# A new spread of the work over the sections of a seven-product attention and mixture kernel, with independent last writes and a root for the first 1/rms

## The chip, the cores and the metric

The kernel runs on one core of a Trainium2 chip. The metric is the device time of one execution in microseconds (us). Three executions of the kernel before gave 538.40, 540.46 and 545.57 us; the time before is their median, 540.46 us.

## What is computed

The reference is an attention block with normed queries and keys, followed by a mixture-of-depths block over the concatenated heads (8 batches, 12 heads, 448 tokens, 64 channels each):

```
q_n, k_n = x / sqrt(mean(x*x) + 1e-6) * g          # for q and for k, per token and head
attn = softmax(q_n @ k_n.T / 8)                    # 448 x 448, for each of 96 heads
x[b, s, :] = concat over heads of attn @ v         # 448 x 768 per batch
scores = x[b] @ w_gate                             # one number per token
top = the 128 tokens with the highest scores       # per batch
out[b] = x[b]
out[b, top] += sigmoid(scores[top]) * (relu(x[b, top] @ w1) @ w2)    # 768 -> 1024 -> 768
```

All data are float32.

## The kernel before

**Attention.** The heads are worked in 24 groups of four heads, three groups to a batch (`n`, `q` in the code; counted from 0). A group has seven units, one for each 64 keys. A unit is `scores` (K times Q into two PSUM banks of the ring `ps_sc`, four banks in all), two `Exp` on ScalarE that write a tile `p`, and `values` (`p` times V, added up over the group in `ps_av`). The 1/rms of the keys is the scale operand of the `Exp`; that of the queries is multiplied into the transposed queries `qT` ahead of the group's first `scores`. For this, `squares` (ScalarE) and `sum_squares` (a sum on VectorE, a power of -0.5 on GpSimd, L263) give `rinv`, `rows_out` writes it to DRAM, `rows_in` reads it back spread over the partitions (`bc`), and `scale_q` (VectorE, L294) multiplies. `scores` of group n cannot start before `scale_q(n)`. Groups 0 and 1 use `scale_q_early`, which spreads `rinv` by small matmuls (L305).

**Denominators.** `add_probs` adds the `p` tiles of a group on VectorE (L375). `by_array(n)` says how many of the last tiles of a group are left to TensorE instead: `sum_keys` multiplies the sum and each of those tiles by `pick_pair` (L402). Then `invert_sums` transposes, takes reciprocals (`rden`, L418), and `to_tokens` turns the group's output to token order in two halves (transposes L433, multiplication by `rden` L435). The second half shares the one bank `ps_aux` with the denominators, so its transposes wait for `rden`.

**Gate and ranks.** `gate` (VectorE, L463, four products for each of two column ranges), `spread`, `score_rows`, `count` (L504) and `annotate` give each token its rank; `select` writes the 128 chosen rows to DRAM (GpSimd's queue, L531), and `load_selected` fetches them.

**Mixture.** Two batches are worked together with a seven-product (Strassen-like) form of both layers. `mixture(g)` is cut in 15 pieces: the transposes of the selected rows (L617), seven products of layer 1 (L649) and seven of layer 2 (L719). Sums of weight blocks are made once (`mix`, L242), stored to DRAM and fetched through a ring of three buffers. Results go out by indirect writes in GpSimd's queue (L574); the last pair of batches has four of them, and each waits for the one before.

**Order of work.** Each engine and each DMA queue takes its instructions in the order in which the program issues them; there is no scheduler. The loop over groups issues `scores` and `values`. Other work is put in a table by `at(slot, ...)` and issued by `run(upto)`; a slot is a unit's number. Groups 0 to 7 have two places for it, after units 3 and 6; from group 8 on, places lie after the group's units, with up to three mixture pieces between them. `urgent` holds `scale_q`, issued in the second half of the group before. After group 23, the rest of the pieces follow, `ranks_of(7)` among them.

## Time and profile before

| of the profiled execution | |
|---|---|
| its own time | 540.99 us |
| span, first to last instruction | 539.3 us |
| TensorE matmul busy | 490.4 us (91%) |
| VectorE busy | 361.3 us (67%) |
| ScalarE busy | 284.2 us (53%) |
| GpSimd busy | 188.1 us (35%) |
| mean granted TensorE clock | 0.972 |

The busy time of TensorE counts modelled ends of overlapping matmuls, so it says little on its own; a pause shows as idle time before a matmul, given in square brackets in the timeline together with what ended it. A wait put down to "issue" ended by nothing that the profile names. The granted clock is the share of the full TensorE clock in a stretch. A matmul of float32 leaves two records in the trace.

### The profile page before, as it was taken

Reading aid. Unit: us, or ns where it says so; the run is one execution under the profiler, and the core shown is the slowest. Engines: PE = TensorE matmul, PEld = TensorE weight load, DVE = VectorE, ACT = ScalarE, POOL = GpSimd, SP = SyncE. Lnnn points to the kernel's source line nnn. Section 1 sums busy time; section 2 is a strip of 40 time slices with the busy share of each in tenths; the row PEclk is TensorE's granted clock in tenths of the full one; section 3 lists DMA queues with packets and bytes.
Section 4 is the critical chain, followed back from the end, with each engine's and each line's share of the span. In section 5 each row is a group of like instructions: output and inputs, shape, how many; then the busy total and the mean of one; then the engine's idle time right before and its main releaser. Section 6 shows DMA issues by size and latency. Waiting matters only on the chain. (4 is left out here: it accounts for less than half of the span.)

```text
span 539.3 us, 12042 instructions
## 1 busy us (share of the span) xinstructions
PE 490.4 (91%) x4861; PEld 294.5 (55%) x4861; DVE 361.3 (67%) x638; ACT 284.2 (53%) x519; POOL 188.1 (35%) x105
## 2 busy tenths in 40 slices
...
GB/s 312 270 287 219 264 211 270 247 300 291 285 237 103 289 281 165 266 143 306 250 298 192 143 349 260 251 143 318 224 248 141 116 124 112 223 260 87 179 89 33
...
## 3 DMA queue, kind: packets, MB, share of 16 engines
...
## 5 line engine op out<-in xcount | busy, mean ns | idle before, releaser
L344 ACT ACTIVATE p<-sc,rinv 128x448 f32<-128x448 f32 x336 | 187.9, 640 | 108.6 <-PE sc L335 94.2
L263 POOL TENSOR_TENSOR rinv<-ss,neg_half 128x14 f32<-128x14 f32 (+1 forms) x49 | 134.0, 2737 | 216.5 <-DVE ss L262 147.7
L335 PE MATMUL sc<-qT,kT 64*64 64x448 f32 x1344 | 163.4, 552 | 15.7 <-issue 11.1
L359 PE MATMUL av<-p,v 64*64 64x448 f32 x1344 | 155.7, 542 | 0.0
L375 DVE TENSOR_TENSOR sum<-sum,p 128x896 f32<-128x896 f32 x91 | 99.2, 1090 | 17.5 <-ACT p L344 13.5
L335 PEld LDWEIGHTS sc<-qT,kT 64*64 64x64 f32 x1344 | 57.7, 134 | 84.4 <-issue 55.4
L359 PEld LDWEIGHTS av<-p,v 64*64 64x64 f32 x1344 | 62.7, 134 | 66.9 <-issue 60.4
L531 POOL DMA_INDIRECT selected<-x,rank x32 | 36.8, 1151 | 62.6 <-DVE x L523 54.8
L435 DVE TENSOR_TENSOR x<-x_ps,rden 112x512 f32<-112x512 f32 x48 | 32.8, 689 | 32.5 <-PE x_ps L433 30.5
L262 DVE TENSOR_REDUCE ss<-sq 128x14 f32<-128x910 f32 (+1 forms) x49 | 52.4, 1075 | 0.9 <-ACT sq L253 0.9
L253 ACT ACTIVATE sq<-tok 128x896 f32<-128x896 f32 (+1 forms) x49 | 45.1, 937 | 6.2 <-DMA tok<-in_tok_dram 5.1
L463 DVE SCALAR_TENSOR_TENSOR prod<-x,wg 112x448 f32<-112x448 f32 (+1 forms) x64 | 35.7, 558 | 2.1
L433 PE MATMUL x_ps<-ident,xT 128*112 128x128 f32 x192 | 29.6, 279 | 6.5 <-DVE rden L418 6.5
L375 DVE TENSOR_TENSOR sum<-p 128x896 f32<-128x896 f32 x24 | 26.1, 1087 | 10.0 <-ACT p L344 10.0
L294 DVE SCALAR_TENSOR_TENSOR qT<-qT,gg,bc 128x896 f32<-128x896 f32 x22 | 25.2, 1145 | 6.0 <-DMA bc<-rows 4.7
L433 PEld LDWEIGHTS x_ps<-ident,xT 128*112 128x112 f32 x192 | 21.7, 135 | 12.3 <-DVE rden L418 9.1
L504 DVE SCALAR_TENSOR_TENSOR cmp<-score_rows,gate,earlier 112x448 f32<-112x448 f32 x32 | 21.9, 684 | 9.8 <-ACT score_rows L494 8.9
L382 ACT COPY xT<-av 128x448 f32<-128x448 f32 x48 | 23.3, 538 | 9.4 <-PE av L359 9.1
L574 POOL DMA_INDIRECT out_dram<-xe,row x7 | 7.7, 1105 | 50.1 <-DVE xe L583 35.9
L649 PE MATMUL moe_ps<-xeT,ring 128*128 128x128 f32 x192 | 23.1, 277 | 0.9 <-DVE hT L666 0.9
L583 DVE SCALAR_TENSOR_TENSOR xe<-moe_ps,xe 128x384 f32<-128x384 f32 x14 | 8.6, 614 | 22.2 <-PE moe_ps L719 22.2
L649 PE MATMUL side_ps<-xeT,w 128*128 128x128 f32 x192 | 23.1, 277 | 0.0
...
## 6 DMA issues: line engine op xcount, KB each, us to landing
...
```

The source lines that it names most:

```text
L253: nc.scalar.activation(out=sq[:, h, :, 0:D], in_=t[:, h], func=AF.Square, scale=scale)
L262: nc.vector.tensor_reduce(out=ss[:, h], in_=sq[:, h], axis=AX.X, op=OP.add)
L263: nc.gpsimd.tensor_tensor(out=rinv[:, h].rearrange(flat), in0=ss[:, h].rearrange(flat), in1=neg_half.to_broadcast([128, (h.stop - h.start) ...
L335: nc.tensor.matmul(out=scs[hh][D * c : D * (c + 1), 0:S], lhsT=get("kT", n)[r, c, D * i : D * (i + 1)], rhs=get("qT", n)[r, c, :], start=True,
L344: nc.scalar.activation(out=p[:, hh], in_=scs[hh][:, 0:S], func=AF.Exp, scale=rinvs[n, 1][:, hh, i : i + 1],)
L359: nc.tensor.matmul(out=avs[n][c][D * hh : D * (hh + 1), 0:S], lhsT=get("v", n)[r, hh, i, :], rhs=probs[u][r, hh], start=(i == 0), stop=(i ...
L375: nc.vector.tensor_tensor(out=sums[n], in0=probs.pop(u - 1) if begins else sums[n], in1=probs.pop(u), op=OP.add)
L433: nc.tensor.transpose(out=ps[:CP, j, :], in_=t[:, j, :], identity=ident)
L435: nc.vector.tensor_tensor(out=xs[b][:, :, col : col + 128].rearrange("p j (h d) -> p j h d", d=D), in0=ps[:CP].rearrange("p j (h d) -> p j ...
L463: nc.vector.scalar_tensor_tensor(out=prod[:, 0 : cols.stop - cols.start], in0=xs[b][:, j, cols], scalar=1.0, in1=wg[:, cols], op0=OP.mult, ...
L531: w = nc.gpsimd.indirect_dma_start(out=t[:, :], out_offset=bass.IndirectOffsetOnAxis(ap=rank[:, j : j + 1], axis=0), in_=x[:, j, :], in_of ...
L649: nc.tensor.matmul(out=ps[:, 128 * f : 128 * f + n], lhsT=w[:, d, 128 * f : 128 * (f + 1)], rhs=h[:, d, :n], start=first and f == d == 0, ...
```

## The change

The tables at the top of the file now set the order. A slot is a group's number plus a fraction (0.5 and 0.9 for the two places of groups 0 to 7; 0.4, 0.6, 0.75 and 0.9 for those of the later groups).

- `scale_q(n)` moves from the second place of group n-1 to its first. `rows_in` follows `rows_out` directly. Loads, squares and sums get new slots.
- `ARRAY` replaces `by_array`: 14 tiles in all go through TensorE instead of 29, and so VectorE makes 106 additions `sum<-sum,p` instead of 91.
- The gate of batch 1 is worked out by TensorE (`pick_gate`, 8 matmuls for each of its groups, then one small multiplication); the 8 products on VectorE for that batch go.
- The weight mixing is spread by `MIXED` from slot 8.9 to 14.6; gates and rankings are cut in halves with slots of their own.
- The mixture starts in group 9, not 8 (`SKIP`); 34 of its 60 pieces are issued by the end of group 23's loop, before 36. In four groups (`OTHER_BANK`) the second half of `to_tokens` takes a bank of `ps_sc` instead of `ps_aux`.
- In layer 1 the result of product 5 is added from its copy in `hT`. In layer 2 of the first two pairs, product 3 comes ahead of 7.
- Of the last pair's writes, the third and fourth are declared independent of the others, and their row numbers are worked out on GpSimd just ahead of each.
- At the start, 1/rms of group 0 is a `Sqrt` on ScalarE, a reciprocal and one correcting step on VectorE, and no power on GpSimd; the first tokens are loaded by two queues, 12 matmuls of zeros run ahead of the branch and 9 warming transposes instead of 13 behind it; `scale_q_early(1)` is issued at the end of group 0 instead of its middle.

```diff
+ARRAY = (0, 0, 1, 2, 2, 1, 2, 2, 1, 0, 0, 2, 1, 0, 0, 0, 0, 0, 0, 0, 0, 0, 0, 0)
+GATE_PE = {1}
+OTHER_BANK = (12, 14, 15, 21)
+SKIP = ((8, 0), (8, 1), (8, 2), (11, 2), (13, 2), (14, 1), (17, 2), (18, 2), (19, 0), (19, 2),
+ (21, 1), (22, 1), (23, 1), (23, 2))
+MIXED = ((1, 1, 0, 8.9), (1, 1, 1, 9.3), (1, 2, 0, 9.6), (1, 2, 1, 10.3), (1, 3, 0, 10.3),
+ (1, 3, 1, 10.3), (1, 0, 0, 10.9), (1, 0, 1, 11.4), (2, 1, 0, 11.9), (2, 1, 1, 11.9),
+ (2, 2, 0, 12.3), (2, 2, 1, 12.6), (2, 3, 0, 12.6), (2, 3, 1, 13.9), (2, 0, 0, 13.9),
+ (2, 0, 1, 14.6))
+PREPARED = {5: {'sq1': 3.5, 'sum0': 2.92},
+ 6: {'scale': 5.5},
+ 7: {'out': 5.5},
+ 8: {'sum1': 6.9},
+ 10: {'in': 8.92},
...
         self.gcol = pool.tile([128, 2], F32, name="gcol", bufs=1)
+        self.load("tok", 0, 0)
         nc.scalar.dma_start(out=self.gcol, in_=g2)
         neg_half = pool.tile([128, 1], F32, name="neg_half", bufs=1)
         nc.vector.memset(neg_half, -0.5)
...
-        warm = pool.tile([128, 1], F32, name="warm", bufs=1)
-        nc.scalar.activation(out=warm, in_=neg_half, func=AF.Exp)
-        self.neg_half = neg_half
-        self.load("tok", 0, 0)
+        warm = pool.tile([128, 2], F32, name="warm", bufs=1)
+        nc.vector.memset(warm, 1.0)
+        nc.scalar.activation(out=warm[:, 0:1], in_=warm[:, 1:2], func=AF.Sqrt)
+        self.neg_half, self.warm = neg_half, warm
...
+        if (name, n, i) == ("tok", 0, 0):
+            for h, queue in enumerate((self.nc.scalar, self.nc.sync)):
+                queue.dma_start(out=t[:, h], in_=src[:, h])
+        else:
+            self.nc.sync.dma_start(out=t, in_=src)
...
+        ss = sss[0, i]
+        for h in [slice(0, 1), slice(1, 2)] if i == 0 else [slice(0, 2)]:
+            nc.vector.tensor_reduce(out=ss[:, h], in_=sq[:, h], axis=AX.X, op=OP.add)
+
+    def root_first(i):
+        root = norm_pool.tile([128, 2, NI], F32, name="ss", bufs=4)
+        nc.scalar.activation(out=root, in_=sss[0, i], func=AF.Sqrt)
+        return root
...
+        nc.vector.reciprocal(out=root, in_=root)
+        nc.vector.scalar_tensor_tensor(
+            out=rinv, in0=root, scalar=-0.5, in1=ss, op0=OP.mult, op1=OP.mult
+        )
+        nc.vector.tensor_tensor(out=rinv, in0=rinv, in1=root, op=OP.mult)
+        nc.vector.scalar_tensor_tensor(
+            out=rinv, in0=rinv, scalar=1.5, in1=root, op0=OP.add, op1=OP.mult
+        )
+        rinvs[0, i] = rinv
...
     def by_array(n):
 
-        return 2 if n < 14 else 1 if n == n_groups - 1 else 0
+        return ARRAY[n]
...
+        for c in range(2 if n // NG in GATE_PE else 0):
+            for j in range(NJ):
+                nc.tensor.matmul(
+                    out=ps[32 * j : 32 * (j + 1), 0:CP],
+                    lhsT=pick_gate[:, n % NG * 2 + c],
+                    rhs=xTs[n, c][:, j, :],
+                    start=False,
+                    stop=(c == 1),
+                )
...
+        rows, written = [], []
+
+        def find_row(engine, i, k):
...
         def write(i, k):
             c0, c1 = parts_out[i][k]
-            nc.gpsimd.indirect_dma_start(
+            if k > 0:
+                find_row(nc.gpsimd, i, k)
+            w = nc.gpsimd.indirect_dma_start(
                 out=out.flatten_outer_dims().rearrange("r (k c) -> (r k) c", c=c1 - c0),
                 out_offset=bass.IndirectOffsetOnAxis(ap=rows[i][:n, k : k + 1], axis=0),
                 in_=xe[i][:n, c0:c1],
                 in_offset=None,
             )
+            for other in written if k > 0 else ():
+                tc.declare_no_dep(w.ins, other.ins, reason="other columns or other rows")
+            written.append(w)
...
-    slot = [0]
-
-    urgent = {}
+    slot = [0.0]
+    A, END = 0.5, 0.9
+    MID, P0, P1, P2 = 0.4, 0.6, 0.75, 0.9
...
-        s2, s1 = NI * (n - 2), NI * (n - 1)
-        late_rows, late_scale = n - 2 >= FIRST, n - 1 >= FIRST
-        times = [s2 - 2, s2, s2 + 2, s2 + 5] if n > 2 else [0, 0, 5, 7]
+        times = {
+            "sq0": n - 3 + (END if n - 3 < FIRST else P0),
+            "sum0": n - 3 + END + 0.03 if n - 3 < FIRST else n - 2 + MID,
+            "sq1": n - 2 + A if n - 2 < FIRST else n - 2 + P0 if n - 3 < FIRST else n - 3 + P1,
+            "sum1": n - 2 + END + 0.02 if n - 2 < FIRST else n - 2 + MID,
+            "out": n - 2 + (A if n - 2 < FIRST else P0),
+            "in": n - 2 + (A if n - 2 < FIRST else P2),
+            "scale": n - 1 + (A if n - 1 < FIRST else P0),
+        }
...
+        for k, t in PREPARED.get(n, {}).items():
+            times[k] = t
         for i in range(2):
-            at(times[2 * i], lambda i=i: sq.setdefault(i, squares(n, i)))
-            at(times[2 * i + 1], lambda i=i: sum_squares(n, i, sq.pop(i)))
-        at(3 if n == 2 else s2 + 3 if late_rows else s2 + 4, rows_out, n)
-        at(5 if n == 2 else s2 + 5 if late_rows else s1, rows_in, n)
-        urgent[s1 + (2 if late_scale else 4)] = n
+            at(times[f"sq{i}"], lambda i=i: sq.setdefault(i, squares(n, i)))
+            at(times[f"sum{i}"], lambda i=i: sum_squares(n, i, sq.pop(i)))
+        at(times["out"], rows_out, n)
+        at(times["in"], rows_in, n)
+        at(times["scale"], scale_q, n)
...
-            at(max(s0 - 26, 4 * (n - 3)), load, "tok", n, 0)
-            at(max(s0 - 26, 4 * (n - 3)), load, "tok", n, 1)
+            for i in range(2):
+                at(n - 5 + P2 if n > 5 else (n - 3) * 0.6, load, "tok", n, i)
         if n > 1:
-            at(max(s0 - 13, 2), load, "qT", n)
-            at(max(s0 - 11, 2), load, "kT", n)
-            at(max(s0 - 11, 2), load, "v", n)
+            at(max(n - 3 + 0.1, 0.3), load, "qT", n)
+            at(max(n - 2 + A, 0.3), load, "kT", n)
+            at(max(n - 2 + A, 0.3), load, "v", n)
...
-            at(16 + 3 * (2 * k + part), load_block, l, b, part)
-    for k, (i, part) in enumerate([(1, 0), (1, 1), (2, 0), (2, 1), (3, 0), (3, 1)]):
-        first = NI * FIRST + k + (3 if i == 3 else 0)
-        at(first, mix, 1, i, part)
-        at(first + 3, store_mixed, 1, i, part)
...
+            at(2.3 + 0.43 * (2 * k + part), load_block, l, b, part)
+    for l, i, part, t in MIXED:
+        at(t, mix, l, i, part)
+        at(t + 0.25, store_mixed, l, i, part)
...
-    for i in range(2):
-        sum_squares(0, i, squares(0, i))
-    later = [squares(1, i) for i in range(2)]
+    sum_first(0, squares(0, 0))
+    root = root_first(0)
+    keys = squares(0, 1)
...
+    invert_first(0, root)
+    sum_first(1, keys)
+    root = root_first(1)
+    nc.scalar.activation(out=loads.warm[:, 0:1], in_=loads.warm[:, 1:2], func=AF.Exp)
     scale_q_early(0)
-    for i in range(2):
-        sum_squares(1, i, later[i])
-
...
     for q in range(n_groups):
         u0 = NI * q
...
                     for u in (i, i + 1):
                         if u in us:
                             scores(u0 + u)
+                        if u0 + u in following:
+                            sum_squares(*following[u0 + u], squares(*following[u0 + u]))
                     run_values(u0 + i - 1 if i < NI - 1 else u0 + i - 2, hold=i == us[2])
-                scale_queries(u0 + us[-1])
-                slot[0] = u0 + us[0]
+                slot[0] = q + (END if place else A)
                 if place == 0:
-                    if q == 0:
-                        scale_q_early(1)
...
+                    if q > NG and g == 1 and b - 1 in GATE_PE:
+                        ranks_of(b - 1)
+                elif q == 0:
+                    scale_q_early(1)
...
                 add_late()
-                run(u0 + us[-1])
+                run(q + (1 - 1e-6 if place else A))
...
                 if u < NI:
                     scores(u0 + u)
             run_values(u0 + i - 1 if i < NI - 1 else u0 + i - 2)
-            if i == 2 and g == 1 and b % 2 == 0:
-                slot[0] = u0 - 2
-                ranks_of(b - 1)
-                run(u0)
-        slot[0] = u0
+            if i == 2:
+                slot[0] = q + MID
+                run(q + MID)
+        slot[0] = q + P0
...
-        next(moe)
-        slot[0] = u0 + 2
-        scale_queries(u0 + 3)
+        run(q + P0)
+        step(q, 0)
+        slot[0] = q + P1
         invert_sums(q - 1)
         to_tokens(q - 1, 0, ps_sc)
-        run(u0 + 3)
-        if q not in (21, 23):
-            next(moe)
-        slot[0] = u0 + 4
-        to_tokens(q - 1, 1, ps_aux)
-        run(u0 + 6)
-        if q not in (10, 11, 13, 15, 17, 19) and q < 20:
-            next(moe)
-        run(u0 + 6)
+        run(q + P1)
+        step(q, 1)
+        slot[0] = q + P2
+        to_tokens(q - 1, 1, ps_sc if q in OTHER_BANK else ps_aux)
+        if g == 0 and b - 1 in GATE_PE:
+            ranks_of(b - 1)
+        run(q + P2)
+        step(q, 2)
...
+            zeros = pool.tile([128, 128], F32, name="zeros")
+            nc.gpsimd.memset(zeros, 0.0)
+            ps = psum.tile([128, 128], F32, name="warm_ps")
+            for _ in range(12):
+                nc.tensor.matmul(out=ps, lhsT=zeros, rhs=zeros, start=True, stop=True)
```

**VectorE in group 4.** `sum<-p` is the first addition of a group, `prod` the gate, `qT<-qT,gg,bc` is `scale_q(5)`, `rden` the reciprocals of the denominators. Before:

```order
L375 TENSOR_TENSOR sum<-p 128x896
L262 TENSOR_REDUCE ss<-sq_122 128x14
L463 SCALAR_TENSOR_TENSOR prod,gate_parts<-x,wg 112x320 x4
L476 TENSOR_REDUCE gate<-gate_parts 112x4
L480 TENSOR_SCALAR parts<-gate 112x4
L481 TENSOR_SCALAR parts<-gate 112x4
L375 TENSOR_TENSOR sum<-sum,p 128x896 x2
L294 SCALAR_TENSOR_TENSOR qT<-qT,gg,bc 128x896
L418 RECIPROCAL rden<-den_ps 112x4x2x2
```

And now:

```order
L435 TENSOR_TENSOR sum<-p 128x896
L354 SCALAR_TENSOR_TENSOR qT<-qT,gg,bc 128x896
L545 SCALAR_TENSOR_TENSOR prod,gate_sums<-x,wg 112x320 x4
L558 TENSOR_REDUCE gate<-gate_sums 112x4
L567 TENSOR_SCALAR parts<-gate 112x4
L568 TENSOR_SCALAR parts<-gate 112x4
L435 TENSOR_TENSOR sum<-sum,p 128x896 x2
L487 RECIPROCAL rden<-den_ps 112x4x2x2
```

`scale_q` stands ahead of the gate and of the two additions, no longer behind them; a sum of squares has left this place.

**TensorE after the last group.** `row_ps` is the start of the ranking of batch 7; `xeT_ps<-ident,p` needs the rows selected by it; each `moe_ps` or `side_ps` row is one product. Before:

```order
L488 MATMUL row_ps<-ident,gate 112x112 x4
L719 MATMUL side_ps<-w_10_179,hT 128x384 x4
L719 MATMUL moe_ps<-ring,xeT 128x384 x4
L719 MATMUL side_ps<-ring,xeT 128x384 x4
L719 MATMUL moe_ps<-ring,xeT 128x384 x4
L719 MATMUL side_ps<-w_11_180,hT 128x384 x4
L719 MATMUL moe_ps<-ring,hT 128x384 x4
L617 MATMUL xeT_ps<-ident,xe 128x128 x6
L617 MATMUL xeT_ps<-ident,p 128x128 x6
```

And now:

```order
L575 MATMUL row_ps<-ident,gate 112x112 x4
L744 MATMUL moe_ps<-xeT,ring 128x128 x12
L814 MATMUL moe_ps<-w_00_191,hT 128x384 x4
L814 MATMUL side_ps<-w_10_192,hT 128x384 x4
L814 MATMUL moe_ps<-ring,xeT 128x384 x4
L814 MATMUL side_ps<-ring,xeT 128x384 x4
L814 MATMUL moe_ps<-ring,xeT 128x384 x4
L814 MATMUL side_ps<-w_11_193,hT 128x384 x4
L814 MATMUL moe_ps<-ring,hT 128x384 x4
L720 MATMUL xeT_ps<-ident,xe 128x128 x6
L720 MATMUL xeT_ps<-ident,p 128x128 x6
```

Eight products stand between the two, before it were six.

**GpSimd's queue at the end,** with the semaphores that each row waits for. Before:

```order
L574 DMA out_dram<-xe,row_5322 3584x768 [waits DMASW7_49,DMASW6_49,DVE_49]
L574 DMA out_dram<-p,row_5334 7168x384 [waits DMASW7_49,DMASW4_49,DMASW0_49]
L574 DMA out_dram<-p,row_5334 10752x256 [waits DMASW1_49,DMASW0_49,DVE_49]
L574 DMA out_dram<-p,row_5334 21504x128 [waits DMASW2_49,DMASW1_49,DVE_49]
```

And now:

```order
L674 DMA out_dram<-xe,row_5261 3584x768 [waits DMASW7_49,DMAHW5_49,DMASW6_49,DVE_49]
L674 DMA out_dram<-p,row_5273 7168x384 [waits DMASW7_49,DMASW4_49,DMASW0_49]
L661 TENSOR_SCALAR row_5273<-p 128x1
L674 DMA out_dram<-p,row_5273 10752x256 [waits DMASW1_49,DVE_49,Pool_49]
L661 TENSOR_SCALAR row_5273<-p 128x1
L674 DMA out_dram<-p,row_5273 21504x128 [waits DMASW2_49,DVE_49,Pool_49]
```

The last two writes no longer wait for the semaphore of the write ahead of them; the second one still does, and a small instruction precedes each of the last two.

## Rows read from the trace of the kernel before

**Rows 1.** Busy time by stretch of the span: start:end, length, then for each engine the busy us and the number of records, the granted clock, the DMA engines' busy share and GB/s. The first four stretches are groups 0 to 7, 9 to 14, 15 to 22, and group 23 with what follows up to the last matmul.

```profile
core 0: us, PE busy (x) PEld busy (x) DVE busy (x) ACT busy (x) POOL busy (x), PEclk, DMA share, GB/s
11.00:134.30 123.30, 110.65 (x1340) 54.88 (x1340) 83.92 (x141) 86.45 (x155) 61.27 (x31) 0.99 0.81 264
155.00:285.20 130.20, 124.17 (x1261) 73.96 (x1259) 95.23 (x166) 70.61 (x129) 44.60 (x22) 0.97 0.71 238
285.20:433.70 148.50, 145.67 (x1396) 84.65 (x1395) 121.77 (x211) 90.78 (x168) 51.86 (x25) 1.00 0.65 213
433.70:525.10 91.40, 84.52 (x571) 62.32 (x570) 40.55 (x86) 19.16 (x37) 11.59 (x12) 0.96 0.46 153
...
304.00:325.20 21.20, 21.20 (x215) 14.59 (x214) 19.91 (x42) 13.70 (x25) 6.80 (x4) 1.00 0.95 331
68.60:87.00 18.40, 15.56 (x174) 7.76 (x174) 11.04 (x22) 11.34 (x21) 5.34 (x2) 0.91 0.73 223
484.40:490.00 5.60, 5.54 (x32) 5.54 (x33) 1.86 (x6) 0.96 (x2) 0.96 (x1) 0.61 0.19 75
```

**Rows 2.** Timeline of TensorE in group 3: start us, duration us, engine, line, operation, names, shapes, count of records.

```profile
53.38 1.71 PE L359 MATMUL av<-p,v 64*64 64x448 f32 x16
54.89 1.71 PE L335 MATMUL sc<-qT,kT 64*64 64x448 f32 x16
...
58.03 0.59 PE L402 MATMUL den_ps<-sum,pick_pair 128*32 128x112 f32 x16
58.44 0.95 PE L402 MATMUL den_ps<-p,pick_pair 128*32 128x112 f32 x32
```

**Rows 3.** Timeline of the first `scores` of groups 4, 5, 7 and 8 (the idle time before them in brackets), with the work on VectorE ahead of that of group 4.

```profile
65.17 2.28 DVE L375 TENSOR_TENSOR sum<-sum,p 128x896 f32<-128x896 f32 x2
67.37 1.15 DVE L294 SCALAR_TENSOR_TENSOR qT<-qT,gg,bc 128x896 f32<-128x896 f32 x1
68.62 1.58 PE L335 MATMUL sc<-qT,kT 64*64 64x448 f32 x8 [3.29 <-issue]
...
87.00 0.98 PE L335 MATMUL sc<-qT,kT 64*64 64x448 f32 x8 [2.82 <-issue]
...
117.96 1.31 PE L335 MATMUL sc<-qT,kT 64*64 64x448 f32 x9 [2.85 <-issue]
...
134.29 1.74 PE L335 MATMUL sc<-qT,kT 64*64 64x448 f32 x16 [2.16 <-issue]
```

**Rows 4.** Timeline: transposes of `to_tokens` that waited for the reciprocals, in groups 11 and 21.

```profile
222.68 1.10 PE L433 MATMUL x_ps<-ident,xT 128*112 128x128 f32 x4 [2.48 <-DVE rden L418]
...
415.02 0.65 PE L433 MATMUL x_ps<-ident,xT 128*112 128x128 f32 x4 [1.93 <-DVE rden L418]
```

**Rows 5.** Timeline after the last group: the ranking of batch 7, two products of layer 2 that follow each other, the last of the four writes of the selected rows, the matmuls that need them, and two products of layer 1.

```profile
462.45 0.59 PE L488 MATMUL row_ps<-ident,gate 112*112 112x112 f32 x4 [0.57 <-DVE gate L476]
...
468.05 2.74 PE L719 MATMUL side_ps<-ring,xeT 128*128 128x384 f32 x8
...
470.63 2.74 PE L719 MATMUL moe_ps<-ring,xeT 128*128 128x384 f32 x8
...
472.67 0.94 POOL L531 DMA_INDIRECT selected<-x,rank  x1 [0.30 <-issue]
...
484.46 1.54 PE L617 MATMUL xeT_ps<-ident,p 128*128 128x128 f32 x6 [5.27 <-DMA p<-selected]
...
492.55 2.84 PE L649 MATMUL moe_ps<-hT,ring 128*128 128x128 f32 x24
...
495.23 2.84 PE L649 MATMUL side_ps<-hT,ring 128*128 128x128 f32 x24
```

**Rows 6.** Timeline of the end: the last result on VectorE and the four writes in GpSimd's queue.

```profile
522.95 0.96 POOL L574 DMA_INDIRECT out_dram<-xe,row  x1 [35.87 <-DVE xe L583]
...
525.10 0.35 DVE L583 SCALAR_TENSOR_TENSOR p<-moe_ps,p 128x128 f32<-128x128 f32 x1 [1.25 <-PE moe_ps L719]
528.86 0.96 POOL L574 DMA_INDIRECT out_dram<-p,row  x1 [4.95 <-DMA out_dram<-xe,row]
532.45 0.96 POOL L574 DMA_INDIRECT out_dram<-p,row  x1 [2.63 <-issue]
535.58 0.96 POOL L574 DMA_INDIRECT out_dram<-p,row  x1 [2.17 <-issue]
```

**Rows 7.** Groups of instructions by line: the gate products, the weight mixing (one of its two groups) and the table load on ScalarE: count | busy us, mean ns of one | idle us before.

```profile
L463 DVE SCALAR_TENSOR_TENSOR prod<-x,wg 112x448 f32<-112x448 f32 (+1 forms) x64 | 35.7, 558 | 2.1
...
L242 DVE TENSOR_TENSOR ring<-ring,w 128x768 f32<-128x768 f32 x8 | 7.3, 952 | 0.0
...
L40 ACT ACT_TABLE_LOAD x1 | 1.3, 1283 | 1.2 <-PEq L1483 1.2
```

**Rows 8.** Two lines by themselves, with min/median/max duration in ns: the additions on VectorE and the power on GpSimd.

```profile
L375 DVE TENSOR_TENSOR sum<-sum,p x91: 1075/1092/1166, 22.1 to 453.1; 128x896 f32<-128x896 f32 x91
...
L263 POOL TENSOR_TENSOR rinv<-ss,neg_half x49: 1474/2581/4095, 6.2 to 419.6; 128x14 f32<-128x14 f32 x47, 128x7 f32<-128x7 f32 x2
```

**Rows 9.** Timeline of the start: the warming transposes, the squares of group 0 and the scaling of its queries.

```profile
4.67 2.95 PE L163 MATMUL warm_ps<-ident 128*128 128x128 f32 x13 [4.67 <-DVE pick_pair L156]
...
4.85 2.04 ACT L253 ACTIVATE sq<-tok 128x448 f32<-128x448 f32 x3 [2.16 <-DMA tok<-in_tok_dram]
...
10.27 1.27 DVE L314 SCALAR_TENSOR_TENSOR qT<-qT,gg,sc 128x448 f32<-128x448 f32 x2 [2.24 <-PE sc L305]
```

228 lines of the change are left out of this document (147 added, 81 removed).

## The prediction

> **What bounds the kernel now.** I read the stretches first [rows 1]. In groups 15 to 22 TensorE is busy 145.67 of 148.5 us, so it bounds that half: 2.8 us of pauses are all that can be won there. Groups 0 to 7 are different: 110.65 of 123.3 us, with neither VectorE (83.92) nor ScalarE (86.45) full, so 12.7 us of TensorE's time are waits. Groups 9 to 14 pause for 130.2 - 124.17 = 6.0 us, the tail for 91.4 - 84.52 = 6.9 us. Next come the causes, from the timelines. In group 4, two additions on VectorE start at 65.17, `scale_q` stands behind them at 67.37 for 1.15 us, and the first `scores` start 0.1 us after its end, having waited 3.29 us [rows 3]. TensorE has nothing else to issue by then. Groups 5, 7 and 8 show 2.82, 2.85 and 2.16 us at the same place. In groups 11 and 21 the transposes wait 2.48 and 1.93 us for the reciprocals [rows 4]. In the tail, TensorE waits 5.27 us for the selected rows [rows 5]. The end is four writes, each behind the one before, while the last result is there at 525.10 + 0.35 [rows 6].
>
> The sum goes against the profiled execution's own 540.99 us, which is 0.5 above the median of the runs, so 0.5 comes off at the end.
>
> **1. Work removed from TensorE and put on it.** 15 of 29 denominator tiles leave. One costs 58.44 - 58.03 = 0.41 us (16 records) [rows 2], so 6.1 us go. The gate of batch 1 adds 8 matmuls, 16 records, to each of three groups; at the same price that is 1.2 us. Every one of these matmuls stood in the stream that sets the pace, except where it lay beside a wait: -4.9, between -3 and -6. VectorE pays 15 additions of 1.09 us, 16.4 us [rows 8], and loses 8 gate products of 0.558 us, 4.5 us [rows 7]. Whether these fit is the question of parts 2 and 3.
>
> **2. Earlier `scale_q` in groups 3 to 8.** Now it stands ahead of the gate and of two additions. The four waits of rows 3 add up to 11.1 us. After such a wait the clock drops as well: 68.6 to 87.0 had 0.91 [rows 1], and 18.4 x 0.09 = 1.7 us. So 12.8 us are to be had. What could be late next: VectorE itself, with 6 of the 15 additions here and the 8 products gone, 83.92 + 6.5 - 4.5 = 85.9 us in some 112, 77%; and ScalarE, 86.45 us in 112, 77%, whose `Exp` are the sole source of `values`. From 304.0 to 325.2 VectorE was busy 19.91 of 21.2 us and TensorE did not pause at all [rows 1], so 77% alone is no obstacle; the order was. `rows_in` now stands directly behind `rows_out` on SP's queue, which can hold the loads behind it back while the row is written; these are for groups two ahead. I take -11, with -5 (half of the waits come back in front of some other operand) and -14 as ends.
>
> **3. Groups 9 to 14.** To be had are 6.0 us of pauses, and 130.2 x 0.03 = 3.9 us of clock (0.97 [rows 1]). But VectorE gets 7 more additions (7.6 us), and by the new table three more mixes of 0.952 us [rows 7] fall in this stretch: 95.23 + 7.6 + 2.9 = 105.7 us in about 125, 85%. The nearest row of a fuller VectorE is again 94% without a pause on TensorE; the row of this stretch itself is 73% with 6 us of pauses. The order has changed for the better (the second half of `to_tokens` has another bank in groups 12 and 14, the mixes are spread), so I lean to the first: -5, between -10 and +8.
>
> **4. Groups 15 to 22.** Pauses of 2.8 us, 1.93 of them the wait in group 21 [rows 4], where the transposes no longer need the bank of the denominators: -1.5, between 0 and -2.8.
>
> **5. The tail.** From `row_ps` (462.45) to the start of `xeT_ps<-ident,p` (484.46) pass 22.01 us, of which TensorE worked 22.01 - 5.27 = 16.74 [rows 5]. The new order puts eight products there, not six: one more of layer 1, 495.23 - 492.55 = 2.68 us, and one more of layer 2, 470.63 - 468.05 = 2.58 us. 16.74 + 5.26 = 22.00: the cover is now as long as the ranking, with nothing to spare. The two products only move, from the stretch of the groups or from behind the wait; their work is in both kernels. With the wait go the cold matmuls behind it, 5.60 us at 0.61 [rows 1], 5.6 x 0.39 = 2.2 us. So up to 7.5; I take -7, with 0 as the other end: the ranking runs through ScalarE, VectorE and two DMAs, and if something stands in its way there, the wait grows by as much.
>
> **6. The last writes.** The second write still waits for the semaphore of the first, and that wait ended last (4.95 us, for the landing). The third and fourth were issued 532.45 - 528.86 = 3.59 and 3.13 us after the one ahead; they now need the write's own 0.96 us on GpSimd [rows 6] and a one-column instruction each, which no row prices; the additions of a full tile take 1.09 us on VectorE [rows 8], the result of 128 columns 0.35 us [rows 6]; I take the smaller, some 0.3. So 2 x 1.26 = 2.5 in place of 6.7 us: -4, between -3 (1.09 each, with the 0.96) and -5.5 (the landing of the last comes sooner too, since no other is under way).
>
> **7. The start.** The power on GpSimd for group 0 (1.47 us at the least [rows 8]) gives way to a root on ScalarE and four small instructions on VectorE; a table load for `Exp`, 1.28 us [rows 7], is now ahead of the first `Exp`, but behind it the queries are still to be scaled, 1.27 us [rows 9]. The 12 matmuls of zeros cost 2 records each; 13 transposes took 2.95 us, 0.227 each [rows 9], so twice 12 x 0.227 = 5.4 us at most, beside the load that the squares wait for (they began at 4.85). I take 0, from -1 to +1.2.
>
> **Sum.** -4.9 - 11 - 5 - 1.5 - 7 - 4 + 0 = -33.4; 540.99 - 33.4 - 0.5 = 507.1, **507 us**. All terms at their better ends give 494, all at their worse ones 539.
>
> **The rivals.** A measurement of this kernel tells about 2% from no change: faster is below 529.7, slower above 551.3.
>
> *The tail keeps its wait.* The products ahead of the ranking are late, or the write and the fetch of the selected rows queue behind other transfers: part 5 is 0. 507 + 7 = 514. For it: the cover has 0 us to spare. Against: the ranking's instructions are the same. 0.14.
>
> *VectorE holds groups 9 to 14.* It runs there no fuller than before, 95.23/130.2 = 0.73: 105.7/0.73 = 144.8, +14.6 in place of -5: 527. For it, the pauses of that stretch at 0.73; against, the 94% of 304.0 to 325.2. 0.08.
>
> *The waits only move.* Parts 2 to 5 give nothing, because each wait on `scale_q` comes back as one on `Exp`, on the bank or on the row fetched by DMA, whose engines were busy 0.81 of groups 0 to 7 [rows 1]. Then only removed work and the writes count: 540.5 - 4.9 - 4 = 531.6. 0.06.
>
> *Slower than before.* `scale_q` of groups 9 to 23 comes late, because it waits in VectorE's order behind additions which themselves wait for the last `Exp` of a group. Each group then pays as groups 4, 5, 7 and 8 did, 11.1/4 = 2.78 us: 15 x 2.78 = 41.7, and the 6.5 us of parts 3 and 4 are not won: 507 + 41.7 + 6.5 = 555. It decides once VectorE's last sums of a group end after TensorE's last mixture piece of that group. The pieces are there as a cushion (two or three of 2.6 us per group, [rows 5]), which speaks against it. 0.03.
>
> *An addition and a power exclude each other.* If an addition on VectorE that starts during a power on GpSimd had to wait until it ends, the new additions would cost more than their own time: 6 in groups 0 to 7 with GpSimd busy 61.27/123.3 = 0.50 of the time, 7 in groups 9 to 14 with 0.34 [rows 1], times a power of 2.58 us [rows 8]: 7.7 + 6.1 = 13.8, and 521. Against it: of 91 additions the longest took 1.166 us, the shortest 1.075, beside powers of up to 4.1 us [rows 8]; no addition waited out a power while it ran. What varies is the power, so if anything the price falls on GpSimd, which has room. 0.03. The Trainium skill states such an exclusion on its page "SBUF — State Buffer", section "SBUF: two separate sides": a VectorE instruction with two operands in SBUF and a GpSimd instruction that reads SBUF take the shared ports in turn, each for the whole instruction, whichever starts first. By that rule the time would be about 521; in the durations of the additions this trace does not bear it out.
>
> *Better than forecast.* Parts 2, 3 and 6 near their better ends: below 497. 0.06.
>
> **Chances and range.** That leaves 0.60 for the forecast, 497 to 516 about its middle. 492 to 525 takes in the tail's rival, the exclusion and most of the better case; outside lie the cases at 527, 532 and 555 and a little beyond either end. Faster by over 2%: all but the case at 532, the slower one and a little of the one at 527, 0.88. Within 2%: 0.09. Slower: 0.03.
>
> **What would show it.** Part 1: 14 denominator tiles on TensorE, and VectorE busy some 16.4 - 4.5 = 12 us more in all. Part 2: no pause above 1 us ahead of the first `scores` of groups 3 to 8, and group 8 starting some 11 us sooner than at 134.29. Part 3: stretch of groups 9 to 14 at about 125 us, VectorE near 85%; a longer one with pauses "<-DVE" means the second rival. Part 4: no wait on `rden` in group 21. Part 5: under 1 us ahead of `xeT_ps<-ident,p` and no stretch at 0.6 of the clock. Part 6: the last two writes some 1.3 us apart, still about 5 us between the first two. Part 7: group 0 begins at about 11 us as before [rows 1]. The prediction is wrong if VectorE's order, not TensorE's stream, sets the length of groups 9 to 14, or if loads that are now issued later hold the first groups.

## The result and the profile after

The changed kernel takes 514.49 us (median of 4 runs, 513.07 to 515.48), the kernel before beside it 539.49 us: a ratio of 0.951, 95% interval 0.944 to 0.959. It is faster by 25 us, where 33 were forecast; 514.5 lies in the stated range of 492 to 525, 7.4 us above the forecast of 507.1. The profiled execution took 514.74 us with a span of 513.0, against 540.99 and 539.3 before: 26.2 us less.

The stretches that answer to [rows 1], in the same columns (start:end, length, then PE, PEld, DVE, ACT and POOL busy us, clock, DMA share, GB/s); each begins with the first `scores` of a group:

```profile
13.16:132.83 119.67, 108.27 (x1292) 53.30 (x1292) 82.57 (x128) 86.58 (x156) 60.57 (x28) 1.00 0.76 250
149.51:270.19 120.68, 117.93 (x1132) 69.21 (x1131) 103.66 (x172) 71.28 (x130) 52.48 (x22) 0.99 0.77 260
270.19:415.51 145.32, 145.32 (x1406) 86.62 (x1405) 121.70 (x209) 90.87 (x170) 52.34 (x25) 1.00 0.70 230
415.51:503.93 88.42, 87.00 (x603) 66.52 (x602) 44.14 (x94) 20.13 (x39) 12.02 (x12) 1.00 0.49 163
```

In groups 15 to 22 TensorE no longer pauses (145.32 of 145.32 us). Groups 9 to 14 are 9.5 us shorter, although VectorE is busy 103.66 us of them in place of 95.23. Groups 0 to 7 are only 3.6 us shorter, and 11.4 us of their 119.67 are still without work on TensorE. Group 8, which lies between the first two of these stretches, took 16.7 us in place of 20.7. Two products of layer 1 and one set of transposes have left it (some 6.7 us, at 2.68 and 1.3 us each), so it lost 2.7 us in other ways, most of it in a wait ahead of its last transposes:

```profile
148.91 0.67 PE L517 MATMUL x_ps<-ident,xT 128*112 128x128 f32 x4 [2.29 <-DVE rden L487]
```

Groups 0 to 7 are where the forecast went wrong, and the first `scores` of groups 3, 4, 5, 7 and 8 say at which places [rows 3]:

```profile
55.05 0.98 PE L395 MATMUL sc<-qT,kT 64*64 64x448 f32 x8 [1.89 <-issue]
...
69.02 0.98 PE L395 MATMUL sc<-qT,kT 64*64 64x448 f32 x8
...
84.64 0.56 PE L575 MATMUL row_ps<-ident,gate 112*112 112x112 f32 x4 [1.76 <-DVE gate L558]
85.13 0.98 PE L395 MATMUL sc<-qT,kT 64*64 64x448 f32 x8
...
117.18 0.98 PE L395 MATMUL sc<-qT,kT 64*64 64x448 f32 x8 [3.26 <-issue]
...
132.83 0.98 PE L395 MATMUL sc<-qT,kT 64*64 64x448 f32 x8 [1.79 <-issue]
```

Groups 4 and 5 lost their pauses of 3.29 and 2.82 us, though TensorE now waits 1.76 us for the gate of batch 0 just ahead of group 5. Groups 7 and 8 kept theirs (2.85 and 2.16 before), and group 3 has one of 1.89. What they wait for shows in the list of VectorE's waits (total us, times, longest); before the change the same list gave 4.7 us to this cause. Six of the eight waits belong to groups 2 to 8, the others to groups 10 and 22:

```profile
DVE qT L354 <- DMA bc<-rows: 24.6, 8, 5.6
```

`scale_q` now stands early in VectorE's order, and the row that it multiplies with is not there yet. Its path for group 7, in the timelines of GpSimd (the powers, L323), of SP's queue (`rows_out` L334, `rows_in` L345) and of VectorE:

```profile
92.78 1.16 POOL L618 DMA_INDIRECT selected<-x,rank  x1 [12.66 <-DVE x L610]
...
97.21 1.75 POOL L618 DMA_INDIRECT selected<-x,rank  x1 [0.30 <-issue]
98.98 10.48 POOL L323 TENSOR_TENSOR rinv<-ss,neg_half 128x14 f32<-128x14 f32 x4
...
101.41 0.52 SPq L99 DMA_DIRECT2D v<-in_vp_dram  x1
104.40 0.38 SPq L334 DMA_DIRECT2D rows<-rinv  x1
111.35 1.11 SPq L345 DMA_DIRECT2D bc<-rows  x2
...
115.92 1.15 DVE L354 SCALAR_TENSOR_TENSOR qT<-qT,gg,bc 128x896 f32<-128x896 f32 x1 [5.64 <-DMA bc<-rows]
```

The powers stand behind four indirect writes in GpSimd's queue; `rows_out` is issued when the power ends, behind the loads of `qT`, `kT` and `v`. It needs 7 us to land, and `rows_in` another 4.5. VectorE waits 5.64 us, and the additions queue behind it. The `v` load shown took 9.7 us to land, so it landed at 111.1, and `rows_out` 0.2 us after it.

The tail, with the matmuls that answer to [rows 5]:

```profile
443.57 0.59 PE L575 MATMUL row_ps<-ident,gate 112*112 112x112 f32 x4 [0.43 <-DVE gate L558]
444.00 2.86 PE L744 MATMUL moe_ps<-xeT,ring 128*128 128x128 f32 x24
...
465.41 0.82 PE L720 MATMUL xeT_ps<-ident,p 128*128 128x128 f32 x6
466.07 2.84 PE L744 MATMUL moe_ps<-xeT,w 128*128 128x128 f32 x24
```

Eight products fill the 21.8 us from `row_ps` to the transposes; these follow without a pause and at full clock (0.82 us for six, 1.54 before). The ranking itself has become quicker as well: the fetch of the selected rows is issued 13.0 us after `row_ps` (at 456.55), where it was 16.6 before. The last writes [rows 6]:

```profile
501.83 0.96 POOL L674 DMA_INDIRECT out_dram<-xe,row  x1 [33.49 <-DVE xe L686]
506.24 0.96 POOL L674 DMA_INDIRECT out_dram<-p,row  x1 [3.46 <-DMA out_dram<-xe,row]
507.24 0.20 POOL L661 TENSOR_SCALAR row<-p 128x1 int32<-128x1 f32 x1
507.71 0.99 POOL L674 DMA_INDIRECT out_dram<-p,row  x1 [0.28 <-POOL row L661]
...
509.24 1.00 POOL L674 DMA_INDIRECT out_dram<-p,row  x1 [0.28 <-POOL row L661]
```

Between the last three lie 1.5 us each. The last matmul's record ends at 503.93, and 9.1 us later the span is over; before, 525.06 to 539.28 were 14.2.

And the start [rows 9]:

```profile
1.05 5.32 PE L1569 MATMUL warm_ps<-zeros 128*128 128x128 f32 x24 [1.05 <-POOL zeros L1566]
...
6.53 1.05 ACT L290 ACTIVATE sq<-tok 128x448 f32<-128x448 f32 x2 [3.34 <-PE warm_ps L1569]
...
13.16 1.34 PE L395 MATMUL sc<-qT,kT 64*64 64x448 f32 x8 [0.77 <-DVE qT L374]
```

The squares began at 4.85 us before; now they wait for the matmuls of zeros, and group 0 begins 2.2 us later.

### The profile page after: what moved, and what is told of

The parts are those of the page before. It is cut to its first block, busy times and chain, and to the rows that moved or that the text cites. A ratio compares the mean times of both kernels' runs of the same rounds, so it can differ in the third digit from the quotient of the medians.

```text
span 513.0 us, 11721 instructions
## 1 busy us (share of the span) xinstructions
PE 482.0 (94%) x4689; PEld 292.9 (57%) x4689; DVE 373.3 (73%) x648; ACT 284.8 (56%) x523; POOL 192.5 (38%) x105
## 4 chain that ended last, share of the span: by engine, by line
PE 51%; DVE 2%; DMA 1%; POOL 1%; issue 1%; POOLq 0%; DVEq 0%
PE sc L395 12%; PE av L419 12%; PE moe_ps L814 7%; PE moe_ps L744 6%; PE side_ps L814 6%; PE side_ps L744 4%; PE x_ps L517 2%; PE den_ps L462 1%; PE xeT_ps L720 1%; DMA out_dram<-xe,row 1%; POOL out_dram L674 1%; PE row_ps L575 1%; DVE prod L545 0%; DVE ring L284 0%; PE den_ps L485 0%
## 5 line engine op out<-in xcount | busy, mean ns | idle before, releaser
L323 POOL TENSOR_TENSOR rinv<-ss,neg_half 128x14 f32<-128x14 f32 x46 | 130.1, 2842 | 158.6 <-DVE ss L322 125.4
L395 PE MATMUL sc<-qT,kT 64*64 64x448 f32 x1344 | 155.5, 547 | 9.8 <-issue 6.9
L419 PE MATMUL av<-p,v 64*64 64x448 f32 x1344 | 149.4, 537 | 0.0
L435 DVE TENSOR_TENSOR sum<-sum,p 128x896 f32<-128x896 f32 x106 | 115.9, 1094 | 4.8 <-ACT p L404 0.2
L395 PEld LDWEIGHTS sc<-qT,kT 64*64 64x64 f32 x1344 | 57.1, 134 | 75.7 <-issue 51.3
L618 POOL DMA_INDIRECT selected<-x,rank x32 | 41.9, 1309 | 94.9 <-DVE x L610 87.6
L322 DVE TENSOR_REDUCE ss<-sq 128x14 f32<-128x910 f32 x46 | 48.6, 1093 | 3.6 <-ACT sq L290 3.6
L354 DVE SCALAR_TENSOR_TENSOR qT<-qT,gg,bc 128x896 f32<-128x896 f32 x22 | 25.3, 1149 | 24.6 <-DMA bc<-rows 24.6
L545 DVE SCALAR_TENSOR_TENSOR prod<-x,wg 112x448 f32<-112x448 f32 (+1 forms) x56 | 31.2, 557 | 1.4
L814 PE MATMUL moe_ps<-ring,xeT 128*128 128x384 f32 x64 | 22.2, 490 | 1.5 <-DVE xeT L696 1.5
```

The source lines that it names most:

```text
L322: nc.vector.tensor_reduce(out=ss, in_=sq, axis=AX.X, op=OP.add)
L323: nc.gpsimd.tensor_tensor(out=rinv.rearrange(flat), in0=ss.rearrange(flat), in1=neg_half.to_broadcast([128, 2 * NI]), op=OP.pow,)
L395: nc.tensor.matmul(out=scs[hh][D * c : D * (c + 1), 0:S], lhsT=get("kT", n)[r, c, D * i : D * (i + 1)], rhs=get("qT", n)[r, c, :], start=True,
L419: nc.tensor.matmul(out=avs[n][c][D * hh : D * (hh + 1), 0:S], lhsT=get("v", n)[r, hh, i, :], rhs=probs[u][r, hh], start=(i == 0), stop=(i ...
L435: nc.vector.tensor_tensor(out=sums[n], in0=probs.pop(u - 1) if begins else sums[n], in1=probs.pop(u), op=OP.add)
L618: w = nc.gpsimd.indirect_dma_start(out=t[:, :], out_offset=bass.IndirectOffsetOnAxis(ap=rank[:, j : j + 1], axis=0), in_=x[:, j, :], in_of ...
```

## The experiments

They ran in three batches, each batch on one chip. The kernel before took 547.30, 543.98 and 546.27 us (medians) in the three, so times are compared within a batch, and across batches by their ratio to the kernel before or by stretches of the trace. (The expectations put some of the pauses about 0.2 us higher than the rows of the matmuls have them.)

The pauses differ from one execution to the next. Five profiles have the changed kernel's order in groups 3 to 8: the two of the changed kernel, and those with the edits to the start, the tail and the last writes below. The stretch took 94.0 to 98.4 us in them, the pause ahead of group 7 was between 0 and 4.6 us, and that ahead of group 8 between 0 and 2.3. In the one without a pause at group 7, group 5 took 18.7 us at a granted clock of 0.91, against 13.9 at 1.00 in the first profile, so TensorE came too late to meet the late row. A single pause that is gone therefore shows little; the length of the stretch and VectorE's waits show more.

**What groups 3 to 8 wait for: two edits, one at a time.** `rows_out` ahead of the loads:

```diff
             times[k] = t
+        if 2 < n < 10:
+            times["out"] = n - 2 + 0.05
```

> The changed kernel with rows_out of groups 3 to 9 issued ahead of the loads of qT, kT and v, not behind them. Theory, the path of the rows ends last (rows_out of group 3 is issued at 40.99 us, 5.8 us after its power has ended, lands after 8 us, then rows_in lands 4 us later, and scale_q waits 4.27 us on VectorE): the pauses ahead of the first scores of groups 3 and 8 (2.06 and 1.96 us) fall below 0.5, that of group 7 (3.42) stays, because its power ends late; the time falls by 3 to 4 us, to about 511. Rival, VectorE's or ScalarE's own work sets these groups: scale_q starts sooner but the pauses come back at other matmuls of the same groups; 514 to 515.

508.78 us, ratio 0.932 (0.923 to 0.941), against 0.951 and 0.946 of the changed kernel in its two measurements. The pauses ahead of the first `scores` of groups 3 and 8 are gone, group 7's stays at 4.47. The wait of 1.76 us for the gate ahead of group 5 is gone too. VectorE waits 9.7 us for rows in all, where it was 24.6:

```profile
DVE qT L354 <- DMA bc<-rows: 9.7, 3, 6.9
...
114.50 1.03 PE L395 MATMUL sc<-qT,kT 64*64 64x448 f32 x4 [4.47 <-issue]
```

The gain is larger than expected: 6.2 us by the spans (506.8 against 513.0), of which 1.65 is a sooner group 0 in this profile, 1.3 fall in groups 3 to 8 (93.2 us) and 3 in groups 9 and 10 (20.0 and 20.9 us, before the edit 21.6 and 22.3), where VectorE no longer waits 3.66 us for the row of group 10. For group 7 the delay only moved. Its power ends at 100.8 here, behind the four indirect writes, and `rows_out` goes at once; but `rows_in`, issued at 104.66 behind the loads of `qT`, `kT` and `v`, brings the row for 113.24. From the power's end to `scale_q` pass 12.4 us, where it was 11.6 without the edit. What is left to win for that group is the power's place in GpSimd's queue.

`scale_q` back in the second place:

```diff
             times[k] = t
+        if 2 < n < 9:
+            times["scale"] = n - 1 + END
```

> The changed kernel with scale_q of groups 3 to 8 in the second place of the group before, as before the change. Theory, the move of scale_q won something in the groups where the row is there in time: pauses of 2 to 3 us ahead of the first scores in groups 4, 5, 7 and 8 again, 519 to 523. Rival, only the arrival of the row counts since the change: scale_q late costs nothing, because the row comes at the end of the group anyway, and the additions that it no longer holds up come sooner; 513 to 516.

531.49 us, ratio 0.973 (0.963 to 0.983): 12 to 15 us slower than the changed kernel, by the ratios, and more than either theory said. First `scores` of groups 4 and 8 on TensorE, and VectorE ahead of group 4:

```profile
68.08 2.29 DVE L435 TENSOR_TENSOR sum<-sum,p 128x896 f32<-128x896 f32 x2
...
73.25 1.14 DVE L354 SCALAR_TENSOR_TENSOR qT<-qT,gg,bc 128x896 f32<-128x896 f32 x1
...
74.50 0.86 PE L395 MATMUL sc<-qT,kT 64*64 64x448 f32 x4 [2.89 <-issue]
...
151.92 1.02 PE L395 MATMUL sc<-qT,kT 64*64 64x448 f32 x4 [4.76 <-issue]
```

All six groups wait, for 2.89 to 4.76 us; groups 3 and 6 had paused only 0.74 us before the change. The rows are there in time (VectorE waits 1.1 us for them in the whole run, where it was 24.6), so it is VectorE's order that ends last here. Groups 3 to 8 take 112.6 us at a granted clock of 0.89, against 103.2 at 0.98 in the kernel before: with the additions that are now in it, a late `scale_q` costs more than it did there. So the move of `scale_q` is worth its place; the row's arrival is what ends last once it is made.

**GpSimd's queue.** The four indirect writes put behind the powers, alone:

```diff
-                times = [q + END] * 3 + [q + 1 + A]
+                times = [q + END, q + END, q + 0.95, q + 1 + A]
```

> The changed kernel with the choice of batch 0's rows put behind the powers of that place (4.90 to 4.95) and nothing else. Theory: the powers start near 89 to 92 us in place of 98.98, rows_out of group 7 is no longer issued at 104.40 but at 100 to 102, behind the loads ahead of it on SP's queue, and the pause ahead of group 7 (3.42, 4.68 and 4.75 us in three profiles) falls below 2.5 us; the pauses of groups 3 and 8 stay. Rival, the queue of loads on SP alone made group 7 late: its pause stays above 3 us.

A miss. The powers start 9 us sooner, as expected, and the pause stays at 4.81 us (a single run, 511.11 us); that of group 8, which was expected to stay, is gone in this profile:

```profile
90.20 5.59 POOL L323 TENSOR_TENSOR rinv<-ss,neg_half 128x14 f32<-128x14 f32 x2 [11.45 <-DVE ss L322]
...
98.31 0.73 SPq L99 DMA_DIRECT2D v<-in_vp_dram  x1
99.14 0.60 SPq L334 DMA_DIRECT2D rows<-rinv  x1
108.95 1.10 SPq L345 DMA_DIRECT2D bc<-rows  x2
...
114.68 0.84 PE L395 MATMUL sc<-qT,kT 64*64 64x448 f32 x4 [4.81 <-issue]
```

`rows_out` stands behind the loads of `qT`, a weight block, `kT` and `v` and then takes 9.8 us until `rows_in` can be issued; it landed 0.2 us after the `v` load ahead of it, at 108.9. Either edit alone leaves group 7 waiting (4.47 and 4.81 us); the two causes lie one behind the other.

**Both, with the start mended as well:**

```diff
-            for _ in range(12):
+            for _ in range(1):
...
+            times["out"] = n - 2 + 0.05
...
+                times = [q + END, q + END, q + 0.95, q + 1 + A]
```

> The changed kernel with three edits together: 1 matmul of zeros, rows_out of groups 3 to 9 ahead of the loads, and the choice of batch 0's rows put behind the powers of that place in GpSimd's queue (its annotate and select from slot 4.90 to 4.95). Theory: the pause ahead of group 7 (3.42 us, 4.63 with rows_out first) comes from powers that stand behind four indirect writes in GpSimd's queue (92.78 to 98.96 us); with them first, rows_out of group 7 is issued before 98 in place of 104.40 us and that pause falls below 1 us; with 2 us of the start and 3 to 4 us of the other rows the time is 8 to 11 us shorter than the changed kernel's. Rival: the choice of the rows, now later, holds the mixture of the first pair, or the pause of group 7 stays because DMA lands late; 3 to 6 us shorter.

502.43 us, against 515.27 for the changed kernel on the same chip (the base of this batch): 12.8 us less, ratio to the kernel before 0.923 (0.918 to 0.928). Expected for the base:

> The changed kernel without an edit, as the base for the other runs on this chip. Theory: the stages are the same as in its first profile; only the start may differ, since the 12 matmuls of zeros took 5.32, 4.88 and less in three profiles; 510 to 519.

Its group 0 began at 13.04 us, and its pauses were those of the first profile, with 4.5 us ahead of group 7. Between the two profiles, 2.4 us are the sooner group 0, 1.2 fall in groups 0 to 2, 8.1 in groups 3 to 8 (90.3 in place of 98.4 us) and 2.8 in groups 9 to 14, while the end takes 1.4 us more. In the combined kernel group 7 no longer waits, group 8 does:

```profile
92.73 0.38 SPq L334 DMA_DIRECT2D rows<-rinv  x1
...
97.25 1.22 SPq L345 DMA_DIRECT2D bc<-rows  x2
...
106.78 0.61 PE L395 MATMUL sc<-qT,kT 64*64 64x448 f32 x4
...
122.21 1.15 DVE L354 SCALAR_TENSOR_TENSOR qT<-qT,gg,bc 128x896 f32<-128x896 f32 x1 [5.59 <-DMA bc<-rows]
...
123.46 1.02 PE L395 MATMUL sc<-qT,kT 64*64 64x448 f32 x4 [2.83 <-issue]
```

**The DMA engines.** From the combined kernel, the layer-2 weights fetched later:

```diff
-            at(2.3 + 0.43 * (2 * k + part), load_block, l, b, part)
+            at(2.3 + 0.43 * (2 * k + part) if l == 1 else 8.7 + 0.25 * (2 * k + part - 8), load_block, l, b, part)
```

> The combined kernel with the six loads of layer-2 weights (512 KB each) moved from groups 5 to 7 to the end of group 8 and group 9. In the combined kernel the row of group 8 is fetched at 113.45 and lands after 122, and the DMA engines are busy 0.91 of groups 3 to 8. Theory, the full DMA engines make the rows land late there: with 3 MB less, the pause ahead of group 8 (2.99 us) falls below 1 us and the time by 2 to 3 us. Rival, the place of the fetch behind the loads of its own group in the queue does it: the pause stays above 2 us and the time is the same; or the weights are late for the mixture: pauses at the products of groups 11 and 12 and a longer time.

> The combined kernel (1 matmul of zeros, rows_out of groups 3 to 9 first, the choice of batch 0's rows behind the powers) without a further edit, as the base of this chip: 499 to 506.

497.84 us against 504.41 for the combined kernel on the same chip: 6.6 us less, where 2 to 3 were expected, and the fastest version tried (ratio to the kernel before 0.915, 0.909 to 0.921). Groups 3 to 8 without and with the edit, in the columns of rows 1:

```profile
49.26:137.32 88.06, 83.89 (x1044) 40.79 (x1043) 69.96 (x118) 65.39 (x119) 43.59 (x20) 0.98 0.94 294
...
119.15 1.15 DVE L354 SCALAR_TENSOR_TENSOR qT<-qT,gg,bc 128x896 f32<-128x896 f32 x1 [5.07 <-DMA bc<-rows]
```

```profile
50.46:134.89 84.43, 82.11 (x1042) 39.81 (x1043) 70.38 (x118) 64.51 (x119) 43.56 (x20) 1.00 0.90 278
...
116.94 1.15 DVE L354 SCALAR_TENSOR_TENSOR qT<-qT,gg,bc 128x896 f32<-128x896 f32 x1 [1.22 <-DMA bc<-rows]
...
119.68 0.61 PE L395 MATMUL sc<-qT,kT 64*64 64x448 f32 x4
```

The row of group 8 arrives in time, VectorE waits 1.22 us for it, not 5.07, and TensorE not at all; the stretch is 3.6 us shorter, at a granted clock of 1.00 in place of 0.98. `rows_in` of group 8 is issued at almost the same time in both (110.56 and 110.78), so it is the transfer that became shorter, with fewer loads around it. The profile lists the six loads with 384 KB each, 2.25 MB together, not the 512 KB and 3 MB of the expectation. The other 3 us of the medians the traces don't show: the two profiled executions took 500.5 and 498.2 us.

**The start.** One matmul of zeros in place of 12, alone:

> The changed kernel with 1 matmul of zeros at the start in place of 12. Theory: the squares, the memsets and the identity of group 0 wait for the last matmul of zeros (its end was 6.37 us, the first squares at 6.53, before the change at 4.85). With one, the squares begin when their tokens are there, near 4.5; group 0 begins at about 11.2 in place of 13.16 us, and the time falls by 1.7 to 2.2 us, to about 512.5. Rival a, the token load ends last: group 0 at 12.9 or later, 514.5. Rival b, the zeros keep the clock up: group 0 begins sooner, but groups 0 to 2 are longer by as much, 514.5.

```profile
1.05 0.80 PE L1569 MATMUL warm_ps<-zeros 128*128 128x128 f32 x2 [1.05 <-POOL zeros L1566]
...
4.00 1.04 ACT L290 ACTIVATE sq<-tok 128x448 f32<-128x448 f32 x2 [0.80 <-DVEq L1586]
...
10.59 1.94 PE L395 MATMUL sc<-qT,kT 64*64 64x448 f32 x14 [0.77 <-DVE qT L374]
```

The squares begin at 4.00 us, and group 0 at 10.59: 2.6 us sooner. The five profiles with one matmul of zeros began group 0 at 9.84 to 10.64 us, the eight with twelve at 10.96 to 13.20, so the cost of the zeros at the start is 0.3 to 3.4 us, depending on the execution. Rival b, a lower clock behind the start, shows in this profile (groups 0 to 2 took 43.14 us at 0.96, 41.89 at 1.00 in the changed kernel), but not in the other four with one matmul of zeros (39.4 to 40.7 us at 1.00). Part of the gain is lost at the other end: from the last matmul to the end of the span pass 10.5 us in all five, and 9.0 to 9.1 in the eight with twelve (but for the one with chained writes), because the second of the last writes waits 4.9 us in place of 3.5. Why that depends on the start no run shows. In the time the edit is not resolved: 511.76 us, ratio 0.938 (0.929 to 0.948), which overlaps with that of the changed kernel.

**The tail.** 36 pieces by the end of group 23, in the changed kernel and then in the combined one:

```diff
- (21, 1), (22, 1), (23, 1), (23, 2))
+ (21, 1), (23, 1))
```

> The changed kernel with 36 of the 60 mixture pieces issued by the end of group 23, as before the change, not 34. Theory: six products instead of eight stand between the ranking of batch 7 and the matmuls that need it; the pause ahead of these is back at 5.0 to 5.5 us, with a stretch at about 0.6 of the clock behind it, and the time is 6 to 8 us longer, about 521. Rival, the ranking is faster or the two products fit somewhere else for nothing: a pause under 1 us, 514 to 516.

> The combined kernel with 36 of the 60 pieces issued by the end of group 23, not 34. Theory, part 5: the pause ahead of the matmuls of the selected rows is back, with a stretch of a lower clock. The earlier run of this edit showed 2.41 us in its profile, the kernel before 5.27, so the pause is 2.4 to 5.5 us and the time 3 to 8 us longer than the combined kernel. Rival: the two products cost nothing in their new places or in the old: within 1.5 us.

In the first, the time was 522.61 us, but the runs lay between 515.78 and 524.92, and the profile, of the fastest, had a pause of 2.4 us only; its interval (0.950 to 0.970) overlaps with the changed kernel's. The second is clearer: 509.95 us against 504.41, 5.5 us more. All its four runs (508.33 to 514.90) lie above the four of its base (500.50 to 507.28), though the intervals of the two ratios (0.929 to 0.941 and 0.922 to 0.933) still overlap, and the pause and the slow matmuls behind it are in the profile:

```profile
461.38 1.54 PE L720 MATMUL xeT_ps<-ident,p 128*128 128x128 f32 x6 [5.72 <-DMA p<-selected]
462.71 4.96 PE L744 MATMUL moe_ps<-xeT,w 128*128 128x128 f32 x24
```

**The last writes** without the declared independence:

```diff
-            for other in written if k > 0 else ():
-                tc.declare_no_dep(w.ins, other.ins, reason="other columns or other rows")
```

> The changed kernel with the last writes depending on each other again. Theory, part 6: from the end of the last matmul to the end of the span pass 13 to 14.2 us in place of 9.09, and the time is 4 to 5 us longer. Rival, the last landing sets the end however the writes are issued: under 1.5 us.

520.36 us against 515.27: 5.1 us more, just above the expectation. The intervals of the ratios overlap (0.948 to 0.961 and 0.941 to 0.952), but the profile shows the same size: the last three writes start 4.95 and 3.26 us after one another, not 1.5 each, and from the last matmul to the end of the span pass 14.3 us, not 9.1.

```profile
506.53 0.96 POOL L674 DMA_INDIRECT out_dram<-p,row  x1 [3.47 <-DMA out_dram<-xe,row]
...
511.48 0.99 POOL L674 DMA_INDIRECT out_dram<-p,row  x1 [3.75 <-DMA out_dram<-p,row]
...
514.74 1.00 POOL L674 DMA_INDIRECT out_dram<-p,row  x1 [2.01 <-DMA out_dram<-p,row]
```

**The denominators.** The tiles on TensorE as before the change:

```diff
-ARRAY = (0, 0, 1, 2, 2, 1, 2, 2, 1, 0, 0, 2, 1, 0, 0, 0, 0, 0, 0, 0, 0, 0, 0, 0)
+ARRAY = (2,) * 14 + (0,) * 9 + (1,)
```

> The changed kernel with the denominator tiles left to TensorE as before the change, 29 and not 14. Theory, part 1 of the prediction: 15 x 0.41 = 6.1 us more on TensorE, of which some 2 us lie in pauses that the fewer additions on VectorE shorten (transposes on rden in group 8, 2.46 us; sums in group 3, 1.04 us): 3 to 6 us longer than the changed kernel. Rival, VectorE is the bound of groups 0 to 14 since the additions were put on it: with 13 fewer there the pauses go, and the time is the same or shorter by up to 4 us.

517.13 us against 515.27, with intervals that overlap: 1.9 us more, below the first theory and not resolved. The price of a tile shows in groups in which the two profiles differ by nothing else: with two tiles more, group 1 took 13.35 us in place of 12.59, group 11 19.01 in place of 18.24 and group 14 18.31 in place of 17.55; with one more, group 13 took 18.65 in place of 18.27. That is 0.38 us for a tile. Groups 9 to 14 took 126.10 us against 120.08 in the base, most of it (4.4 us) in group 9, which ran at a granted clock of 0.87. Groups 3 to 8 took 94.50 against 98.35, but the changed kernel's first profile had 94.46 there with the new tiles, so no cost of the additions is shown.

## Why the prediction was right, and where not

| Part | Forecast, us | Measured |
|---|---|---|
| 1. denominators, gate | -4.9 | 0.38 for a tile, 0.41 forecast; -1.9 in the time, not resolved; the gate was not tried alone |
| 2. groups 0 to 7 | -11 | about -2.3 |
| 3. groups 9 to 14 | -5 | about -6.2 |
| 4. groups 15 to 22 | -1.5 | -3.2, with one set of transposes (1.3) more |
| 5. tail | -7 | -3.0 with two products (5.3) more; pause and slow clock gone; -5.5 by experiment |
| 6. last writes | -4 | -5.1, in the profile and by experiment |
| 7. start | 0 | +2.2 |
| group 8, no term | 0 | -4.0, with two products and one set of transposes (6.7) less |

By stretch, the profiled execution became shorter by 3.6 us (groups 0 to 7), 4.0 (group 8), 9.5, 3.2, 3.0 (group 23 and behind it) and 5.1 (last writes), and longer by 2.2 at the start: 26.2 us in all. Part 1 lies within these. VectorE is busy 12.0 us more in all (373.3 against 361.3), as part 1 said.

**Part 2 failed,** and makes the difference. Groups 0 to 7 became 3.6 us shorter, and part 1 has a share of 6 x 0.41 - 1.2 = 1.3 us in that; group 8 starts 1.5 us sooner (132.83), where 11 were forecast. The step read: "What could be late next: VectorE itself [...] and ScalarE", and of `rows_in` only that it "can hold the loads behind it back". The working went by what `scale_q` stands behind on VectorE and left out when its operand arrives. Before, `rows_in` of group 4 was issued at 57.1 us and took some 4 to land, and `scale_q` started at 67.4; this slack of about 6 us on another queue was not looked up. With `scale_q` half a group earlier, some 7 us, it was used up: the row's path (power, 7 us to land, 4 us to fetch) ends last. The earlier `scale_q` did what the forecast said in group 4 and, but for the 1.76 us that came back as a wait for the gate, in group 5, and undoing it costs more than was forecast for it. The rival "the waits only move" had named "the row fetched by DMA" at a chance of 0.06; it came true for this one part of its four.

**Part 7 failed by its price.** The 5.4 us of zeros were worked out rightly (5.32) and put beside the load of the tokens; but the squares, the identity and the memsets wait for the last of them, the squares for 3.34 us. The bound of +1.2 should have been 6.53 - 4.85 = 1.7 us, and a little more.

**Part 3 held.** 9.5 us shorter, of which 8 tiles less are 3.3. VectorE is at 86% there (85% forecast) and TensorE pauses 2.8 us: the rival of VectorE at 0.73 is refuted. Which of the changes in this stretch did it was not tried one by one. **Part 4** was sized too small; the wait in group 21 is gone, as said, though the bank of its own was not tried alone. **Group 8** had no term: its mixture pieces were moved away, and without them its transposes wait 2.29 us for `rden`.

**Part 5 held** in its mechanism, with more to spare than the forecast had: the ranking became 3.6 us shorter as well, and no pause is left at all. **Part 6** was short by 1.1 us: the distances of 3.59 and 3.13 us went to 1.5 each, 3.7 us in all and within the bounds, and the second write's own wait fell from 4.95 to 3.46 us. This last fall is not the work of the declared independence: the wait is 3.47 us with the chain back, and 4.9 in all profiles with one matmul of zeros.

**The exclusion** of additions and powers did not show: the 106 additions took 1.091 us in the median, 1.467 at most, 1.092 and 1.166 before. Of the 106, 48 started while a power ran on GpSimd, and they took 1.092 us in the median and 1.117 at most. The Trainium skill's rule in "SBUF — State Buffer", section "SBUF: two separate sides", would lengthen them by up to a whole power; the trace does not bear it out on VectorE's side.
